# First segment of a retention and SwiGLU kernel: masks built on the chip from one head's table, the decay split into factors of q or y, of v, and a constant a head, with a new order of the first steps

## The chip, the cores and the metric

The kernel runs on one core of a Trainium2 chip. The metric is the device time of one execution in microseconds (us); smaller is better. A core has TensorE (PE in the profile, with its weight loads as PEld), VectorE (DVE), ScalarE (ACT), GpSimd (POOL), SyncE (SP, which here only issues DMAs), and 16 DMA engines that all transfers share. Each engine works off its own list of instructions in order, and waits for the others by semaphores.

## The reference

Retention with a decay per head, then a SwiGLU feed-forward block on the result:

```python
gamma = 1.0 - 2.0 ** (-5.0 - np.arange(H))
for t in range(S):
    state = gamma * state + k[:, :, t] (outer) v[:, :, t]
    y[:, :, t] = q[:, :, t] @ state / sqrt(D)
x = y.transpose(0, 2, 1, 3).reshape(B * S, H * D)
g = x @ w_gate
out = (silu(g) * (x @ w_val)) @ w_out
```

B = 4, H = 8, S = 768, D = 64; the block has 3072 tokens, 512 columns and 1536 inner columns. q, k and v are 32-bit floats; the weights come as 64-bit floats.

## The kernel before, in words

**Chunks and segments.** A sequence of 768 positions is cut into 6 chunks of 128 (NCK = 6, P = 128). For a chunk, retention is: scores k q for each head, multiplied by a mask that holds gamma^(t-j) for j <= t and 0 elsewhere; the sum of v over the masked scores (the chunk's own part); the product of q, decayed by gamma^(t+1), with the state that the chunks before have left (the old part); and the new state, gamma^128 times the old plus k, decayed by gamma^(127-j), times v. The work goes in four segments of six chunks each: segment 0 has the first three chunks of sequences 0 and 1. Each segment is retention, the up products of the feed-forward block, and the down products. The first segment also has to turn the 64-bit weights into 32-bit ones piece by piece, while it uses them, and stores them for the later segments.

**The order of the work** is written out by hand in PLAN (lines 51 to 232): a list of steps, each of which issues its instructions on all engines when its turn comes. `run()` (line 609) goes through it, and `do()` (line 618) looks each letter up in `parts` (line 595). Steps that PLAN doesn't name would come behind, by due times (LATE, WHEN). The engines themselves then run in the order in which PLAN handed them their instructions.

**DMA queue.** SP issues nearly all DMAs, in PLAN's order, and the first two loads of q go out on ACT's queue. A DMA also waits for the landing of the one eight places ahead of it, so at most eight are in flight.

**The steps that matter here**, with n the place of a chunk in segment 0 (0 and 1 are the first chunks of the two sequences, 2 and 3 the second, 4 and 5 the third):

- `A n` (line 609) loads a part of the table `decays` into the tile `tab`. The table has the masks of all 8 heads (512 KB), qdec (256 KB: the factors for q), kdec and gdec (6 KB). TABS (line 38) cuts it into five loads.
- `l n:w` (load_chunk, line 485) loads k (w = 0), q (1), v (2), each 256 KB, or k by rows (3) of a chunk. `U`, `V` load raw weights (line 532), `Z` stores turned ones (line 503).
- `I` (unit_of, line 684) makes a unit matrix out of the first head's mask; `r` (rows_of, line 687) transposes k of chunks 0 and 1 with it on PE (line 692), so that these two needn't be loaded by rows.
- `s` (scores, line 645): 8 matmuls for the heads (line 651), and two DVE products with the mask (line 657).
- `k`, `K`, `E` (scale_k, scale_k_act, lines 668 to 679): k by rows times kdec, on POOL, on DVE (chunk 0) and as eight ACT operations (chunk 1).
- `q`, `Q` (scale_q, line 662): q times qdec into another buffer, for chunks 2 to 5, on POOL or DVE.
- `o` (mix_old, line 728): the old part. `m` (mix, line 738): the own part (matmuls in line 742) and then `far_a` on ACT (line 1138), the first of three terms into which y is cut for the exact products behind. `x n:1` and `x n:2` (split_x) make the other two on DVE (lines 418 and 1145).
- `t` (state, line 702): matmuls of line 713, then a copy by ACT (line 716, chunks 0 and 1) or an addition by DVE (line 718). `g` (decay, line 699) multiplies the old state by gdec.
- `a b c S C T` turn a raw weight piece (ACT lines 553, 556, 559; DVE lines 566, 574, 418; POOL line 576 for the down weights). `n` (near_0) cuts turned weights into three terms (ACT line 1129, DVE line 1132, POOL line 1135).
- `p`, `v`, `u`, `y`: products of the first two inner columns' blocks for one pair of chunks (PE line 1075), silu (ACT line 1081), and the product of both (DVE line 1086). `G`, `W`, `i`, `j`: the same for a whole segment (PE line 1057, DVE line 463).
- `h0`, `h1` (local_part, line 790) copy halves of the mask into `local` for segment 1, `h2` prepares qdec for it. `L` loads kdec for segment 1 (line 770). `P n` loads k, q or v for segment 1 (load_old, line 928).

Of the kernel before, what the change touches and what calls it, by code (L numbers as in the profile page):

```python
# [14 lines left out]
AF = mybir.ActivationFunctionType  # L15
ALU = mybir.AluOpType
# [21 lines left out]
TABS = 0, QDEC0 // 2, 3 * QDEC0 // 4, QDEC0, KDEC0, NTAB  # L38
# [17 lines left out]
    C0:0 o2 U1:1 m2 o3 n0:3 s4 m3 a1:1 n0:4 x2:1 l5:1 l3:3  # L56
    b1:1 x2:2 x3:1 S1:1 t2 n0:2 p0:0 q4 a1:0 x3:2 c1:1 n0:5 k3
    C1:1 g3 b1:0 n1:0 v0:0 l5:0 U2:3 s5 S1:0 t3 c1:0 C1:0 l5:2
    p0:1 n1:1 u0:0 u0:1 T0:0 q5 v0:1 a2 l4:2 b2 y0:1 o5 y0:0
    o4 n1:3 S2 n1:2 m5 T0:1 n1:4 c2 m4 n1:5 x5:2 p1:0 l5:3  # L60
    x5:1 p1:1 u1:0 C2 v1:0 U3:1 T0:2 x4:2 T1:0 U12:0 a3 v1:1 y1:0
    x4:1 T1:1 L b3 p0:2 a12 c12 n2:0 S3 u1:1 T1:2 b12 u0:2
    U4:3 c3 Z0 n2:1 v0:2 Z1 n2:3 S12 y1:1 a4 n2:2 p1:2 v1:2
    C3 u1:2 n2:4 G2:0 y0:2 C12 G2:1 n3:0 U13:1 y1:2 n3:1 n2:5 b4
    T2:0 n3:2 S4 U5:2 n3:3 c13 T2:1 W2:0 Z12 W2:1 h0 c4 i2:1
    n3:4 i2:0 G3:0 n3:5 T3:0 C4 T2:2 T3:1 U6:3 j2:0 a5 G3:1 T3:2
    j2:1 Z2 n4:0 U7:0 W3:0 i3:0 n4:1 b5 n4:2 n4:3 S5 n4:4 W3:1
# [12 lines left out]
    c16 n10:1 G9:1 Z15 j8:0 j8:1 n10:2 a16 n10:3 t5 U17:2 b16 W9:0  # L80
    i9:1 T9:1 0/h0.0 T9:2 S11 Z8 W9:1 S16 G10:1 n10:4 i9:0 C16 c11
    C11 n10:5 n11:0 j9:0 Z9 G10:0 n11:3 Z16 i10:1 j9:1 a17 i10:0 W10:1
    P1 n11:4 T11:0 T11:1 1/was0.0 T11:2 n11:1 W10:0 Z11 c17 n11:2 n11:5 b17
    0/h0.1 0/W0 G11:1 0/h1.0 G11:0 j10:0 0/d0.0 h1 0/h0.2 1/sc0 j10:1 i11:0 0/h1.1
    0/W1 S17 0/d1.0 i11:1 0/d0.1 1/l3 C17 T10:0 1/dec0.0 W11:0 0/d1.1 0/d0.2 W11:1
    0/h2.0 j11:0 0/D0.2 j11:1 1/k0.0 1/l4 1/dec0.1 1/q0.0 0/D0.1 1/q0.1 0/D0.4 1/k0.1 1/l5
    0/D0.0 0/h2.1 0/d1.2 0/h1.2 0/h4.0 0/W2 0/Z0 1/A0 1/y0.06 1/new0.0 0/h4.1 1/y0.01 0/D0.5
    0/D0.3 0/d2.0 1/B0 0/D1.1 0/h3.0 1/y0.03 0/D1.5 1/y0.04 0/Z1 1/y0.02 1/y0.07 1/y0.05 T10:1
    1/was0.1 1/y0.15 1/y0.00 1/y0.14 0/d2.1 0/D1.4 1/y0.12 0/d2.2 0/D1.2 1/y0.13 0/W3 Z17 0/D1.3
    0/Z2 0/d3.0 0/D1.0 0/h2.2 0/h3.1 1/C0 0/W4 T10:2 0/h3.2 0/d3.1 0/h4.2 Z10 1/y0.16  # L90
    1/l7 1/y0.17 1/new0.1 1/sum0.0 0/D2.3 0/D2.1 1/y0.10 0/h5.0 1/begin 1/sum0.1 0/d3.2 0/h5.1 1/y0.11
    0/D2.5 1/sc1 0/D2.0 0/d4.0 1/was1.0 0/D2.4 0/d4.1 0/D3.4 1/l6 1/dec1.1 0/h5.2 1/dec1.0 0/D2.2
    1/x0.2.0 0/D3.1 1/q1.1 0/d4.2 0/W5 0/D3.5 1/x0.1.0 0/h6.0 1/k1.0 0/Z3 1/sum0.3 1/k1.1 1/sum0.2
    1/x0.2.1 0/D4.5 0/D3.2 0/D3.3 0/D3.0 1/q1.0 0/Z4 0/h6.1 0/D4.0 0/D4.4 1/x0.1.2 1/x0.1.1 1/A1
    1/x0.0.0 0/d5.0 1/x0.2.2 1/y1.00 0/h6.2 1/y1.06 1/x0.0.2 1/new1.0 0/D4.2 0/d5.1 0/d5.2 0/D4.3 0/D4.1
    1/y1.07 1/y1.01 0/W6 0/h7.0 1/B1 1/x0.0.1 1/y1.04 1/y1.12 0/h7.1 1/l9 0/d6.0 0/D5.4 0/h8.0
    0/d6.1 1/y1.02 0/D5.3 0/D5.2 0/W7 0/h8.1 1/y1.05 0/d6.2 1/l8 1/l11 0/Z5 1/y1.03 1/was1.1
    0/D5.5 1/C1 0/d7.0 1/y1.16 0/d7.1 0/D6.5 0/D5.0 1/y1.17 1/y1.15 1/new1.1 0/h7.2 1/y1.14 1/y1.11
    0/D5.1 1/y1.13 1/x1.2.0 0/D6.3 0/d7.2 0/D6.4 0/Z6 1/y1.10 0/D7.3 0/h9.0 1/sc2 0/h8.2 1/x1.2.2
    0/D6.2 1/q2.1 1/k2.1 0/D7.5 0/W8 1/sum1.0 0/D6.1 1/sum1.2 1/k2.0 0/D6.0 0/D7.1 1/x1.1.0 0/h10.0  # L100
    0/h9.1 0/d8.0 0/D7.2 1/dec2.0 1/l10 1/sum1.1 1/dec2.1 0/W9 1/x1.1.1 0/D7.0 0/d8.1 1/x1.2.1 0/Z7
    1/sum1.3 1/was2.0 1/q2.0 1/x1.0.0 1/x1.1.2 0/d9.0 0/D7.4 0/d8.2 0/h11.0 1/A2 1/new2.0 0/D8.0 1/x1.0.1
    0/h10.1 0/D8.3 0/D8.2 0/d9.1 1/L0 0/D8.1 1/y2.00 0/D8.4 1/B2 0/W10 0/d9.2 1/y2.07 1/y2.05
    0/d10.0 0/D8.5 0/h9.2 1/y2.02 0/h11.1 0/D9.3 1/y2.03 0/h10.2 1/y2.01 0/D9.5 0/Z8 1/y2.04 1/y2.06
    1/w0.0.0 0/D9.4 0/d10.1 0/h11.2 1/C2 1/y2.16 1/y2.14 0/W11 1/y2.12 0/D9.1 1/y2.10 0/D9.2 1/L1
    0/d10.2 0/D10.3 0/Z9 0/d11.0 1/y2.17 1/x1.0.2 1/y2.15 1/y2.13 0/D9.0 1/L2 0/D10.4 0/D10.1 1/sum2.2
    0/D10.2 0/D10.0 1/y2.11 0/d11.1 1/sum2.0 0/d11.2 1/x2.1.0 1/sum2.1 1/x2.1.2 1/sum2.3 0/D11.1 0/Z11 1/w0.1.0
    0/D11.0 1/x2.0.0 0/D11.3 0/D10.5 0/D11.4 1/w0.0.1 0/D11.2 1/w0.0.2 1/w1.0.0 1/x2.1.1 1/x2.0.1 0/Z10 1/w1.0.1
    0/e0 0/o0 1/x2.0.2 1/w1.0.2 0/D11.5 1/p0.0 1/u0.0 1/p0.1 1/p0.2 1/p1.0 1/x2.2.0 1/u0.1 1/w0.2.0
    0/e2 0/o2 1/x2.2.1 1/w0.1.1 1/p1.1 1/w1.1.0 1/x2.2.2 1/u0.3 1/w1.2.0 1/u1.0 1/p1.2 1/u0.2 1/w0.2.1  # L110
    1/L3 1/w0.1.2 1/w1.2.1 1/w0.2.2 0/e1 1/p0.3 1/w2.2.0 1/w2.1.0 1/u0.4 0/e3 1/w1.1.1 1/w1.1.2 1/L4
    1/p0.4 1/u1.1 1/u0.5 1/p0.5 2/ta 1/w2.0.0 1/u0.6 1/u1.3 1/p0.6 1/p1.3 1/u1.4 1/u0.8 1/p1.4
    1/p1.5 1/w3.1.0 1/w3.0.0 1/w2.0.1 1/w1.2.2 1/u0.9 1/w2.0.2 1/p2.0 1/u2.0 1/p2.1 1/w2.1.1 1/w2.1.2 1/u1.5
    1/w3.2.0 1/u1.6 1/p1.6 1/w3.1.1 1/u2.1 1/w4.2.0 1/w4.2.1 1/w2.2.1 1/w3.0.1 1/p2.2 1/u1.8 1/u1.2 1/u2.3
    1/p2.3 1/p2.4 1/u2.4 1/u2.5 1/p2.5 1/w4.1.0 1/w4.0.0 1/w3.0.2 1/p3.1 1/u1.9 1/p3.0 1/u2.6 1/w3.1.2
# [1387 lines left out]
```

## Time and profile before

| what | value |
|---|---|
| time, 3 runs | 639.51, 639.64 (median), 640.4 us |
| span of the profiled execution | 641.7 us |
| ACT, POOL busy | 396.6, 173.2 us |
| TensorE clock granted, mean | 0.997 |
| PE's first matmul with data | 5.93 us |
| DMA | 143.03 MB, mean 223 GB/s |

No time of the profiled execution is given beside its span; the span of 641.7 us stands 2.1 us over the median of the runs without a profile. A row of a chain or a timeline begins with its start and its length in us, counted from the start of the span; in a group of instructions the last columns are the busy time in us and the mean of one in ns. PE stands for its matmuls; a matmul of 32-bit floats appears as two records, so 8 of them are x16.

### The profile page before, as it was taken

To read this page: it belongs to the slowest core of one execution; us is meant where nothing else is said; L and a number is where in the kernel's file an instruction comes from. 1 tells how busy PE (TensorE), PEld (TensorE's weight loads), DVE (VectorE), ACT (ScalarE), POOL (GpSimd) and SP (SyncE) were. 2 spreads that over 40 slices of the span, in tenths; PEclk is the share of its full clock that TensorE was granted. 3 is DMA by queue.
4 is the path that set the end of the run, shared out by engine and by line. 5 is a ranking of instruction groups with operands and counts; after the bars stand their busy time and mean duration, and the time that the engine had idled before them with its cause. 6 is when DMAs were issued, how large, how long until landed. Compare 5 with 4: busy or idle time off the path is not lost.

```text
span 641.7 us, 14131 instructions
## 1 busy us (share of the span) xinstructions
PE 630.8 (98%) x5601; PEld 581.7 (91%) x5601; DVE 506.9 (79%) x764; ACT 396.6 (62%) x845; POOL 173.2 (27%) x117
## 2 busy tenths in 40 slices
PE   7999999999999999999899999999999999999997
PEld 6899999987789999997788999998888999999886
DVE  4998788899898889887489777978778888877551
ACT  4786897677866665667376664756764655564220
POOL 0544455544423531210001343340002014232000
PEclk9999999999999999999899999999999999999999
DMA  9899998689788443688783435577785345304764
GB/s 319 289 353 311 372 333 274 259 323 305 281 278 305 140 157 115 214 263 239 204 312 130 179 115 206 173 203 229 229 290 196 113 149 189 128 13 140 230 212 149
DMA packets 57747, 143.03 MB, mean 223 GB/s; under 512 B 5840, under 2 KB 28368, under 8 KB 57680
## 3 DMA queue, kind: packets, MB, share of 16 engines
q1 hardware_dynamic: 57104, 141.33, 64.5%
q8 instruction: 44, 0.72, 0.5%
q10 hardware_dynamic: 576, 0.79, 0.3%
q14 instruction: 23, 0.19, 0.1%
HBM read 112.21 MB, written 29.88 MB: 221 GB/s over the span
## 4 chain that ended last, share of the span: by engine, by line
PE 94%; DMA 5%; ACT 1%; SPq 1%; issue 0%; DVE 0%; ACTq 0%
PE bank L1230 41%; PE bank L1301 30%; PE bank L1057 13%; PE bank L825 5%; PE bank L1075 3%; DMA oitem<-wdnt 2%; DMA hT<-in_v_n_dram 2%; PE bank L742 1%; DMA hT<-in_q_t_dram 1%; PE bank L728 0%; SPq L820 0%; PE bank L713 0%; PE bank L651 0%; ACT gitem L1129 0%; ACT local L871 0%
## 5 line engine op out<-in xcount | busy, mean ns | idle before, releaser
L1301 PE MATMUL bank<-oitem,gitem 128*128 128x512 f32 (+1 forms) x873 | 205.9, 393 | 3.0 <-DMA oitem<-wdnt 2.9
L1301 PEld LDWEIGHTS bank<-oitem,gitem 128*128 128x128 f32 x873 | 161.9, 189 | 38.1 <-DMA oitem<-wdnt 3.5
L1230 PE MATMUL bank<-xa,gitem 128*128 128x384 f32 x864 | 160.6, 334 | 0.0
L1230 PEld LDWEIGHTS bank<-xa,gitem 128*128 128x128 f32 x864 | 150.6, 188 | 0.1
L1135 POOL TENSOR_TENSOR gitem<-gitem 128x768 fp32r<-128x768 f32 x36 | 72.1, 2007 | 185.0 <-DVE gitem L1132 165.7
L1135 POOL TENSOR_TENSOR oitem<-oitem 128x512 fp32r<-128x512 f32 (+1 forms) x48 | 52.8, 1105 | 168.1 <-DVE oitem L1132 148.0
L418 DVE SCALAR_TENSOR_TENSOR gitem<-gitem 128x768 fp32r<-128x768 f32 x84 | 86.6, 1041 | 1.7 <-DVE gitem L1132 0.5
L1057 PE MATMUL bank<-xa,oitem 128*128 128x384 f32 x480 | 84.2, 335 | 0.0
L1230 PE MATMUL bank<-xb,gitem 128*128 128x384 f32 x432 | 83.7, 335 | 0.0
L1057 PEld LDWEIGHTS bank<-xa,oitem 128*128 128x128 f32 x480 | 83.0, 188 | 0.2
L1230 PEld LDWEIGHTS bank<-xb,gitem 128*128 128x128 f32 x432 | 75.8, 188 | 0.4
L1129 ACT ACTIVATE gitem<-loads 128x768 fp32r<-128x768 f32 x72 | 59.1, 842 | 25.7 <-PE bank L1230 16.9
L1132 DVE SCALAR_TENSOR_TENSOR gitem<-gitem,loads 128x768 fp32r<-128x768 f32 x72 | 70.5, 991 | 3.4 <-ACT gitem L1129 3.3
L1132 DVE SCALAR_TENSOR_TENSOR gitem<-gitem,hT 128x768 fp32r<-128x768 f32 x48 | 46.2, 965 | 28.0 <-ACT gitem L1129 24.1
L1129 ACT ACTIVATE gitem<-hT 128x768 fp32r<-128x768 f32 x48 | 40.2, 844 | 43.7 <-PE bank L1301 35.3
L1230 PE MATMUL bank<-xb,oitem 128*128 128x384 f32 x216 | 43.0, 335 | 0.0
L1230 PEld LDWEIGHTS bank<-xb,oitem 128*128 128x128 f32 x216 | 38.0, 188 | 0.0
L1246 ACT COPY tmp<-bank 128x384 f32<-128x384 f32 x36 | 17.3, 480 | 27.0 <-PE bank L1230 22.9
L1247 DVE TENSOR_TENSOR hT<-bank,tmp 128x384 f32<-128x384 f32 x36 | 20.0, 554 | 16.5 <-PE bank L1230 16.4
L1245 ACT COPY tmp<-bank 128x384 f32<-128x384 f32 x36 | 17.2, 479 | 24.8 <-PE bank L1230 17.1
L1249 DVE TENSOR_TENSOR hT<-hT,bank 128x384 f32<-128x384 f32 x36 | 19.7, 550 | 13.4 <-ACT bank L1249 13.2
L1247 ACT COPY tmp<-bank 128x384 f32<-128x384 f32 x36 | 17.3, 481 | 16.5 <-PE bank L1230 11.9
(152 smaller groups left out, 807.2 us busy)
## 6 DMA issues: line engine op xcount, KB each, us to landing
loads<-wup SPq DMA_DIRECT2D x36, 896.0 KB, 5.4
oitem<-wdnt SPq DMA_DIRECT2D x33, 768.0 KB, 4.7
wdnt<-oitem SPq DMA_DIRECT2D x12, 768.0 KB, 5.8
wup<-first SPq DMA_DIRECT2D x9, 896.0 KB, 6.9
rawp<-in_w_gate_dram SPq DMA_DIRECT2D x12, 512.0 KB, 7.3
rawp<-in_w_val_dram SPq DMA_DIRECT2D x12, 512.0 KB, 6.6
rawp<-in_w_out_dram SPq DMA_DIRECT2D x12, 512.0 KB, 5.8
out_dram<-chunk_x SPq DMA_DIRECT2D x21, 256.0 KB, 4.7
```

The source lines that it names most:

```text
L418: stt(o, x, 1.0, y, op0=mul, op1=op)
L825: nc.tensor.matmul(o, a, b, start=start, stop=True, skip_group_check=True)
L1057: nc.tensor.matmul(o, w[:, a, ts(b, P)], X0[:, a, i, NC - 1 - b], start=a == b == 0, stop=a == 2 and b == NC - 1, skip_group_check=True)
L1075: nc.tensor.matmul(o, w[:, a, ts(b, P)], X0[:, a, :, NC - 1 - b, ts(j, P)], start=a == b == 0, stop=a == 2 and b == NC - 1, skip_group_che ...
L1129: act(o[0], x, AF.Copy, scale=CUT / FAR)
L1132: stt(o[1], f32(o[0]), -FAR, x, op0=mul, op1=add)
L1135: op(o[2], f32(o[0]), f32(o[1]), op=add)
L1230: nc.tensor.matmul(o, w[:, a, k], x[:, a, KH - 1 - k], start=start and a == k == 0, stop=a == 2 and k == KH - 1, skip_group_check=True)
L1246: lambda: act(gate, c11, AF.Silu, scale=ONE), lambda: copy(u2, x),
L1247: lambda: copy(p5, wb), lambda: tt(h1, x, p5, op=add),
L1249: lambda: act(x, x, AF.Silu, scale=ONE), lambda: tt(h1, h1, x, op=mul))
L1301: nc.tensor.matmul(o, hs[g][:, a, ds(i * TH + u * P, P)], wo[g][:, a, cols], start=n == 0 and (f == 0 or final), stop=f == NF - 1 and a == ...
```

## The change

Written for one head, with a chunk's positions j and t, the mask is gamma^(t-j) = gamma^(t+1) * gamma^(127-j) * gamma^(-128). The change uses this three times over. Only the first head's mask is loaded (64 KB, into `loads` as `causal`), as a pattern of where j <= t. DVE makes the eight masks out of it: the constant gamma^(-128) of the head where the pattern is not 0, and 0 elsewhere (eight operations of 128 x 128). v is multiplied by kdec in place, on POOL, for all six chunks, and so k by rows stays as it is: the transposed k of chunks 0 and 1 is only copied out of PSUM, by DVE and by ACT. q of chunks 2 to 5 is multiplied by qdec in place, on POOL, ahead of the scores, and the old part reads the same q. Chunks 0 and 1 have no old part: their q stays unscaled, and instead the finished y is multiplied by qdec (`J`, DVE, out of PSUM into `loads`) before it is cut into three terms.

The table comes in three loads: the first mask, qdec, and the rest. The masks for segment 1 are no longer copied by ACT out of `tab`, but loaded from `decays` (`M0`, `M1`). PLAN has a new order up to the first steps of the down stage; from there on it is unchanged.

The core of the diff:

```diff
-TABS = 0, QDEC0 // 2, 3 * QDEC0 // 4, QDEC0, KDEC0, NTAB
+TABS = (0, P), (QDEC0, KDEC0), (KDEC0, NTAB)
...
-    A0 I0 l0:0 l1:0 A2 A1 U0:0 s0 a0:1 r1 l0:2 s1 b0:1
-    A4 A3 l2:1 l2:0 r0 m0 K0 S0:1 c0:1 l1:2 x0:1 t0 s2
-    E1 l3:0 l3:1 m1 l2:3 C0:1 g2 V0:0 a0:0 Q2 n0:0 b0:0 l2:2
-    x1:2 s3 x1:1 n0:1 l4:1 l4:0 l3:2 t1 S0:0 k2 x0:2 q3 c0:0
+    A0 I1 A2 I2 l0:0 I0 l1:0 s0 l0:2 s1 l1:2 U0:0 k0 A1 r0 r1 E1 l2:1 k1 K0 m0 l2:0 a0:1 m1 b0:1 q2
+    J0 l3:1 l3:2 S0:1 l2:2 t0 V0:0 c0:1 J1 x0:1 l3:0 t1 g2 l2:3 C0:1 x1:1 l4:0 s2 n0:0 q3 a0:0 n0:1
+    o2 l4:1 o3 b0:0 x0:2 U1:1 x1:2 S0:0 k2 c0:0 l5:1 n0:2 m2 s3 l5:2 l5:0 C0:0 x2:1 k3 n0:3 p0:0
...
-        "E": lambda n: scale_k_act(cs[n]),
-        "k": lambda n: scale_k(cs[n]), "q": lambda n: scale_q(cs[n]),
+        "E": lambda n: keep_rows(cs[n], act), "K": lambda n: keep_rows(cs[n], tt),
+        "k": lambda n: scale_v(cs[n]), "q": lambda n: scale_q(cs[n]),
+        "J": lambda n: scale_y(cs[n]), "M": lambda n: local_mask(n),
...
+    def scale_q(c, op=pool):
+        qt = pairs(chunks[c][1])
+        op(qt, qt, qdec, op=mul)
+
+    def scale_v(c, op=pool):
+        vn = chunks[c][2].rearrange("p (h d) -> p h d", h=H)
+        op(vn, vn, kdec[:, :, None].to_broadcast([P, H, D]), op=mul)
+
+    def keep_rows(c, engine):
+        (copy if engine is act else nc.vector.tensor_copy)(chunks[c][3], turned.pop(c))
...
+    def unit_of(n):
+        if n == 2:
+            nc.vector.tensor_scalar(unit, causal, 0.124, None, op0=ALU.is_ge)
+            return
+        for m in range(NP):
+            back = (1.0 - 2.0 ** (-5.0 - (2 * m + n))) ** -float(P)
+            nc.vector.tensor_scalar(mask[:, n, m], causal, 2.0 ** -20, back,
+                                    op0=ALU.is_ge, op1=mul)
...
+    def y_of(c):
+        n = cs.index(c)
+        return pairs(loads[:, ts(4 + n, 512)]) if c % NCK == 0 else y_parts(c)[0]
+
+    def scale_y(c):
+        tt(y_of(c), y_parts(c)[0], qdec, op=mul)
+        far_a(x_of(c), y_of(c))
...
-        far_a(x_of(c), y)
+        if c % NCK:
+            far_a(x_of(c), y)
...
+    def local_mask(n):
+
+        nc.sync.dma_start(
+            out=lmask1[half[n]].rearrange("p i n -> p (i n)").rearrange("p (m t) -> p m t", t=HC),
+            in_=decays[half[n], :QDEC0].rearrange("p (m t) -> p m t", t=P)[:, :, half[n]])
```

As the engines get them: PE's list has the same matmuls in a new order (scores 0 and 1, both transposes, mixes 0 and 1, states 0 and 1, scores 2, old parts 2 and 3, mix 2, scores 3, the first 12 matmuls of line 1075, mix 3, state 2, scores 4, 36 more of line 1075, state 3, scores 5, old parts 4 and 5, mixes 5 and 4, and then the 96 of line 1075). SP's list begins with the mask, the small table, k of chunks 0 and 1, v of chunks 0 and 1, the first gate weights, qdec, q and k of chunk 2, q and v of chunk 3, v of chunk 2, the first value weights, k of chunk 3. POOL's begins with v of 0 and 1, q of 2 and 3, v of 2.

More of the change, by code (lines that the diff above doesn't have):

```diff
@@ L608, in tile_retnet_swiglu @@
         "V": lambda n, p: load_piece(pieces[n], p[0], slice(1)), "l": lambda n, p: load_chunk(n, p[0]),
-        "A": lambda n: nc.sync.dma_start(out=tab[:, tabs[n]], in_=decays[:, tabs[n]]),
+        "A": lambda n: nc.sync.dma_start(
+            out=tab[:, tabs[n]] if n else causal, in_=decays[:, tabs[n]]),
         "Z": lambda n: keep_wt(n) if n < NF else keep_dn(n - NF),
@@ L659, in scores @@
         att[c] = a
[L662 to L679 removed]
+    def scale_q(c, op=pool):
[6 more added lines that the diff above has]
+        (copy if engine is act else nc.vector.tensor_copy)(chunks[c][3], turned.pop(c))
     turned = {}
     unit = loads[:, ds(10 * 512, P)]
[L684 to L685 removed]
+    causal = loads[:, ds(10 * 512 + P, P)]
+    def unit_of(n):
[6 more added lines that the diff above has]
+                                    op0=ALU.is_ge, op1=mul)
     def rows_of(n):
@@ L790, in local_part @@
     def local_part(n):
-        if n < 2:
-            copy(lmask1[half[n]].rearrange("p i n -> p (i n)").rearrange("p (m t) -> p m t", t=HC),
-                 mask[half[n]].rearrange("p i n t -> p (i n) t")[:, :, half[n]])
-        else:
-            act(lg1, qdec[:, :, HC - 1], AF.Copy, scale=float(np.sqrt(D)))
-            copy(qdec[:, :, half[1]], qdec[:, :, half[0]])
+        act(lg1, qdec[:, :, HC - 1], AF.Copy, scale=float(np.sqrt(D)))
+        copy(qdec[:, :, half[1]], qdec[:, :, half[0]])
+    def local_mask(n):
+        nc.sync.dma_start(
+            out=lmask1[half[n]].rearrange("p i n -> p (i n)").rearrange("p (m t) -> p m t", t=HC),
+            in_=decays[half[n], :QDEC0].rearrange("p (m t) -> p m t", t=P)[:, :, half[n]])
     def own_rows():
@@ L1427, in tile_retnet_swiglu @@
         made[:, ts(i % 2, 512)] for i in range(6)]
-    tabs = [slice(a, b) for a, b in zip(TABS, TABS[1:])]
+    tabs = [slice(a, b) for a, b in TABS]
     early[20:22] = early[18:20]
```

364 lines of the change are left out of this document (170 added, 194 removed).

## The prediction

> **What bounds the kernel now.** I read the page first, then the chain that ended last in order of time, then the waits of PE.
>
> ```profile
> PE 630.8 (98%) x5601; PEld 581.7 (91%) x5601; DVE 506.9 (79%) x764; ACT 396.6 (62%) x845; POOL 173.2 (27%) x117
> ...
> PE 94%; DMA 5%; ACT 1%; SPq 1%; issue 0%; DVE 0%; ACTq 0%
> ```
>
> PE is 94% of the chain. The DMA share is worth a look: where does PE wait?
>
> ```profile
> 0.73 3.99 DMA hT<-in_q_t_dram
> ...
> 4.74 5.02 DMA hT<-in_v_n_dram
> ...
> 10.63 7.57 DMA hT<-in_v_n_dram
> ...
> 18.24 1.09 PE bank L742 x16
> 19.34 1.02 PE bank L728 x16
> 20.36 1.09 PE bank L651 x16
> ...
> 22.48 0.46 PE bank L713 x16
> 22.94 3.06 PE bank L1075 x24
> ...
> 32.66 1.90 PE bank L742 x32
> 34.56 11.71 PE bank L1075 x96
> 46.27 58.25 PE bank L1057 x336
> ...
> 269.91 13.04 PE bank L1230 x74
> 282.95 0.02 issue
> ```
>
> From 18.24 to 282.95 every piece of the chain is PE's. So the end of the kernel is set by when PE gets through the first segment's retention: whatever it reaches the 96 matmuls of L1075 earlier, the end comes earlier, as long as nothing behind runs dry. Before 18.24 the chain is three DMAs in a row: q of the first chunk lands at 0.73 + 3.99 = 4.72, v of the first chunk at 9.76, v of the third at 18.20.
>
> ```profile
> PE bank L651 <- DMA hT<-in_k_t_dram: 1.7, 2, 1.1
> PE bank L742 <- DMA hT<-in_v_n_dram: 1.4, 2, 0.9
> ...
> PE bank L651 <- DVE tmp L657: 0.4, 1, 0.4
> ```
>
> ```profile
> 5.93 1.16 PE L651 MATMUL bank<-hT 64*128 64x128 f32 x16 [1.14 <-DMA hT<-in_k_t_dram]
> 7.02 0.66 PE L692 MATMUL bank<-loads,hT 128*128 128x128 f32 x4
> ...
> 34.49 11.78 PE L1075 MATMUL bank<-xa,oitem 128*128 128x256 f32 x96
> ```
>
> PE's real work starts at 5.93 and the 96 matmuls at 34.49, 28.56 us later. The waits in between are 1.7 - 1.1 + 1.4 + 0.4 = 2.4 us. That and the start at 5.93 are all that a new front can win.
>
> **PE's work in the front does not change.** By the pitches of the chain: 6 scores at 1.09, 6 mixes (L742) at 1.05 (mean of 1.09 and half of 1.90, rounded up for the tail), 4 products with the old state (L728) at 1.02, 4 states (L713) at 0.5 (0.46 here), 2 transposes at 0.59 (7.02 to 7.61), 4 units of 12 matmuls of L1075 at 1.53 (half of 3.06): 6.54 + 6.30 + 4.08 + 2.00 + 1.18 + 6.12 = 26.2. With 2.4 of waits that is 28.6, as measured. The changed order has the same pieces.
>
> **DMA.** Ahead of PE the loads queue up.
>
> ```profile
> 5.90:18.20 12.30, 10.04 (x152) 8.45 (x152) 9.63 (x15) 7.91 (x22) 2.73 (x2) 1.00 1.07 373
> 18.20:34.49 16.29, 16.25 (x225) 14.92 (x225) 15.40 (x27) 11.55 (x22) 7.66 (x6) 1.00 0.87 292
> 34.49:44.50 10.01, 10.01 (x85) 10.01 (x84) 9.18 (x17) 9.41 (x14) 3.07 (x3) 1.00 0.97 354
> 44.50:55.00 10.50, 10.50 (x67) 10.50 (x67) 10.45 (x15) 8.04 (x12) 6.58 (x4) 1.00 0.90 293
> ```
>
> Behind the length of each window the columns are PE, PEld, DVE, ACT, POOL, then clock, DMA share and GB/s. At 373 GB/s and a share of 1.07 a load of 256 KB takes 0.70 us, one of 512 KB 1.41. The whole table is 792 KB; the change loads 64 KB (one head's mask), 6 KB and 256 KB (qdec): 466 KB or 1.27 us less in this queue. More counts what stands ahead of whom. At 4.72 512 KB have landed. The new issue order is mask, small table, k0, k1, v0, v1, gate weights, qdec, q2, k2, q3, v3, v2, value weights, k3 (with q0, q1 on ACT's queue). Counting 0.70 per 256 KB from 4.72: k0 at 5.61 (838 KB), k1 6.32, v0 7.02, v1 7.72, gate 9.13, qdec 9.83, q2 10.53, k2 11.24, q3 11.94, v3 12.64, v2 13.35, value weights 14.75, k3 15.46. SP now issues k0 behind two tables, not one:
>
> ```profile
> 1.18 0.90 SPq L485 DMA_DIRECT2D hT<-in_k_t_dram  x2
> ```
>
> Two issues take 0.90, so k0's goes from 1.18 to 1.63, and with q's 3.99 from issue to landing that is 5.62, the same. Bounds for k0: 5.1 if the two queues share evenly, 5.9 as now.
>
> One lag has to be added. From v0's 9.76 to the third v stand 2566 KB, 7.02 us, so 16.8; it landed at 18.20, 1.4 late. In that stretch one packet of instructions went through the same engines:
>
> ```profile
> q8 instruction: 1, 0.02, 2.3%
> ```
>
> It will come again at about the same count of PE's instructions, near 14 us in the new order, so I put k3 at 16.9 and everything behind it 1.4 later.
>
> **The other engines' new work.**
>
> ```profile
> L657 DVE TENSOR_TENSOR tmp<-bank,tab 128x512 f32<-128x512 f32 x10 | 6.4, 684 | 3.8 <-PE bank L651 3.8
> ...
> L666 DVE TENSOR_TENSOR loads<-hT,tab 128x512 f32<-128x512 f32 x1 | 1.2, 1242 | 0.0
> ...
> L672 DVE TENSOR_TENSOR hT<-bank,tab 128x512 f32<-128x512 f32 x1 | 0.7, 692 | 0.0
> ...
> L685 DVE TENSOR_SCALAR loads<-tab 128x128 f32<-128x128 f32 x1 | 0.2, 226 | 3.5 <-DMA tab<-in_decays_dram 3.5
> ```
>
> ```profile
> L666 POOL TENSOR_TENSOR loads<-hT,tab 128x512 f32<-128x512 f32 x2 | 3.0, 1504 | 0.0
> L672 POOL TENSOR_TENSOR hT<-hT,tab 128x512 f32<-128x512 f32 x2 | 2.1, 1040 | 14.2 <-DMA hT<-in_k_n_dram 14.2
> L666 POOL TENSOR_TENSOR loads<-first,tab 128x512 f32<-128x512 f32 x1 | 1.3, 1277 | 0.0
> ```
>
> ```profile
> L1138 ACT ACTIVATE xa<-bank 128x512 fp32r<-128x512 f32 x5 | 3.0, 593 | 1.6 <-PE bank L742 1.5
> ...
> L679 ACT ACTIVATE hT<-bank,tab 128x64 f32<-128x64 f32 x8 | 1.7, 332 | 0.0
> ...
> L716 ACT COPY states<-bank 128x256 f32<-128x256 f32 x2 | 0.7, 361 | 0.0
> ```
>
> *Masks.* Eight of the 226 ns operations more on DVE, 1.8 us. The mask is issued where q is, so it lands by 4.72; with the unit matrix that is 4.72 + 2.03 = 6.75, when the first scores come out (5.66 + 1.16): no cost, and what lands later than that is lost one for one.
>
> *v scaled on POOL.* New wait: mix of the first chunk now waits for POOL, 1.04 behind v0: 7.02 + 1.04 = 8.06; the second at 9.10. PE gets there later (below): no cost. It cannot gain. *q scaled before the scores:* 1.28 to 1.50 on POOL behind q2: 12.0; q3 13.5.
>
> *k kept unscaled.* Eight ACT operations (1.7 us) become one of about 0.6, DVE's stays at 0.69: ACT wins 1.1, hidden. *y scaled.* Two DVE operations of 0.68, read from PSUM like L657, each between a mix and the ACT step L1138; the one of the first chunk waits for qdec (9.83). Behind it on DVE stands the weight conversion, behind ACT's L1138 the copy of the first state. DVE's q (1.24) leaves for POOL. DVE in sum: 1.81 + 1.36 - 1.24 = 1.9 us more.
>
> *Late steps.* The mask of the second segment is no longer copied by ACT but loaded twice, 131 KB in 512 rows of 256 bytes. By bytes 0.35 us of the queue each, by a gate load's 512 rows 1.41; the first stands where loads now pause for buffers, the second late with PE supplied. I take the middle, 0.9. Two old k loads (1.4 us) are moved up behind the first, past other weights. The second window's share of 0.87 against 1.07 leaves 0.2 x 16.29 = 3.3 us of DMA time free, which covers these 2.3; uncovered they would hold the next weights by as much.
>
> **PE's path, step by step (start of each).** Scores 0 at 5.66, scores 1 at 6.75, transposes 7.84, mix 0 at 9.02, mix 1 at 10.07, state 0 at 11.12. State 1 overwrites the bank, so it waits for ACT's copy: 11.8 + 0.36 = 12.2, 0.6 idle. Scores 2 at 12.7 (POOL 12.0), old products 13.8 and 14.8 (POOL 13.5), mix 2 at 15.8 (v scaled at 14.4; DVE's products of scores 2: eight operations of 0.65 from mix 0's end at 10.3, so 15.5, tight). Scores 3 at k3's 16.9, 0.05 idle, and then 18.0 first unit of L1075, 19.55 mix 3, 20.6 state 2, 21.1 scores 4, 22.2 three units, 26.8 state 3, 27.3 scores 5, 28.4 two old products, 30.4 mixes 4 and 5. The 96 matmuls begin at 32.4 to 32.5: 5.66 + 26.2 + 0.65. Against 34.49 that is 2.0 to 2.1 us earlier: 0.3 from the start, 1.75 from waits.
>
> **Does it hold behind?** The nearest producers of before:
>
> ```profile
> 42.73 1.30 POOL L1135 TENSOR_TENSOR oitem<-oitem 128x512 fp32r<-128x512 f32 x1 [6.69 <-DVE oitem L1132]
> ...
> 43.70 0.42 DVE L1086 TENSOR_TENSOR hT<-bank,tmp 128x256 f32<-128x256 f32 x1
> ```
>
> POOL's part ends at 44.03; PE takes it after 8 of L1057 (58.25/336 = 0.173) behind 46.3, at 47.7: 3.6 us to spare. DVE's product ends at 44.12 and frees the bank for the last 12 of the 96, at 34.49 + 84 x 0.122 = 44.7: 0.6 to spare, but it follows PE's own results. So 2.1 can be carried. The profile spans 641.7 with nothing around it told; the median of the three runs is 639.64, 2.1 under the span. I take the difference off the median: **637.5**.
>
> **Rivals.** (1) *The start stays a DMA start.* k0 lands at 5.9 as now, and the 1.4 lag falls on q3 and v2: v2 at 14.8, scaled 15.9, mix 2 and all behind 0.6 to 0.9 later. Gain 0.8: 638.8. For it: the share of 1.07; against: 466 KB less.
>
> (2) *DVE hands part of it back.* The far steps of the first two chunks now read y from SBUF together with xa, beside POOL's products. The one such pair in the trace, DVE's L666 and POOL's L666, took 1.24 instead of 0.68 and 1.50 on average instead of 1.28. Two such steps stand ahead of the products of scores 2, so mix 2 would wait for 15.5 + 1.1 = 16.6; two more ahead of those of scores 3, so mix 3 would come up to 1.8 later in all. I take 1.4: 638.9. The Trainium skill, "SBUF — State Buffer", section "Who interferes with whom", states a lock: a VectorE instruction with two SBUF inputs and a GpSimd instruction that reads SBUF exclude each other for a whole instruction. By it each of the four could wait out a POOL product of 1.04 to 1.50, 4.2 to 6.0 in all, which would turn this rival into a loss of 1.7 to 3.5 us if POOL were busy throughout. The pair in this trace agrees in kind, with less.
>
> (3) *Slower: DVE becomes the bound from 18 to 55 us.* There it is busy 15.40 + 9.18 + 10.45 of 36.8 us, 1.77 idle. The change gives it 1.9 and, by (2), 2.2 more, 4.1. If the front takes none of it, DVE ends this stretch 4.1 - 1.77 = 2.4 later than now, and past the 0.6 to spare PE ends 1.8 later than now: 641.5. It decides from the point where less than 1.8 of the 4.1 fits into the front; for it speaks DVE's 95%; against, that DVE idled 2.67 of 12.3 us in the first window and 3.5 before its first operation, where the masks go.
>
> **From the cases to the numbers.** Forecast 637.5 at 0.60, with 636.3 to 638.3 as its own spread, down to 635.6 if k0 lands at 5.1 and no wait is left (5.1 + 26.2 = 31.3, 3.2 earlier) and late POOL slack still holds; rival 1 0.15; rival 2 0.10; rival 3 0.15. Range 635.6 to 639.8: it leaves out rival 3 and little else. Differences under 0.2% (1.3 us) count as the same, about what a measurement of this kernel can tell: faster 0.60, same 0.25, slower 0.15.
>
> **What would show it.** First scores of PE near 5.6; the first mix near 9.0 with POOL's product long done; the third scores waiting for nothing; PE's waits before the 96 matmuls about 0.7 in all; the 96 matmuls at 32.4; no wait of PE from there to its first DMA wait near 281. I am wrong if PE waits for DVE between 18 and 55, if a wait for v or k of the later chunks is as long as now, or if POOL's products take 1.7 each and the scores wait for them.

## The result, and the profile after

Before took 639.74 us (639.51 to 640.4, 4 runs), after 649.62 us (649.18 to 650.36, 4 runs): ratio 1.0156, 95% interval 1.0142 to 1.0171. The change makes the kernel **9.9 us slower**; the forecast was 2.1 faster. (Line numbers of after are 7 lower than those of before near L400 to L600 and 5 higher from L1057 on. In the experiments below they are 15 to 26 lower than in the kernel that each starts from, as the schedule is written on fewer lines; go by engine, tile and count there.)

The page of after, busy times and chain:

```profile
PE 633.6 (98%) x5601; PEld 583.1 (90%) x5601; DVE 519.6 (80%) x773; ACT 393.7 (61%) x836; POOL 178.6 (28%) x120
...
PE 84%; DVE 5%; DMA 5%; issue 2%; ACT 2%; SPq 0%; POOL 0%; ACTq 0%; DVEq 0%; POOLq 0%
```

PE fell from 94% of the chain to 84%. DVE has 9 instructions more, which the prediction put at 1.9 us, but is busy 12.7 us longer. PE's waits up to 290 us (us in total, times, longest):

```profile
PE bank L1306 <- DVE hT L456: 2.1, 1, 2.1
PE bank L1062 <- DVE hT L456: 2.1, 3, 1.2
PE bank L1062 <- POOL oitem L1140: 1.2, 1, 1.2
...
PE bank L1062 <- ACT tmp L456: 1.0, 1, 1.0
PE bank L1062 <- ACT first L552: 0.7, 1, 0.7
```

None of these lines was there before; by the time axis they lie at 60 and 64, 94, 113, 125 to 129, and 139 us. In all PE idles 7.1 us between 35 and 145 us, where before it idled nowhere. PE's own line by time shows that the front did not lose:

```profile
5.85 3.70 PE L646 MATMUL bank<-hT 64*128 64x128 f32 x32 [1.03 <-DMA hT<-in_k_t_dram]
9.49 1.09 PE L686 MATMUL bank<-loads,hT 128*128 128x128 f32 x8
...
21.27 1.53 PE L744 MATMUL bank<-tmp,hT 128*64 128x128 f32 x15 [0.33 <-POOL hT L663]
...
34.39 11.83 PE L1080 MATMUL bank<-xa,oitem 128*128 128x256 f32 x96
```

The 96 matmuls start at 34.39, 0.1 earlier than before. A mark further on is the first product of the down stage (12 in a row on L1301, now L1306). In the chain of before:

```profile
132.41 2.97 PE bank L1301 x12
```

In that of after it comes at 141.10, 8.7 later. So the loss is made between 46 and 141 us:

```profile
46.22 10.42 PE bank L1062 x60
56.69 0.64 ACT oitem L1134
57.35 0.69 DVE oitem L1137
58.04 0.61 DVE first L411
58.68 1.41 DVE first L411
60.11 1.38 DVE first L411
...
84.07 8.40 DMA wup<-first
...
131.16 4.42 DMA oitem<-wdn
...
137.73 2.77 issue
140.50 0.56 DVE hT L456
141.10 4.39 PE bank L1306 x12
```

Where before had PE alone, DVE, ACT and DMAs take turns: the weights of the first segment (converted by ACT and DVE, summed by DVE on L411, stored by SP) arrive just behind PE. At the end, 12 products take 4.39 us in place of 2.97: the clock was halved there (below).

### The profile page after: what moved, and what is told of

Same layout as the page of the kernel before. It is cut to its first block, busy times and chain, and to the rows that moved or that the text cites. A ratio compares the mean times of both kernels' runs of the same rounds, so it can differ in the third digit from the quotient of the medians.

```text
span 647.3 us, 14138 instructions
## 1 busy us (share of the span) xinstructions
PE 633.6 (98%) x5601; PEld 583.1 (90%) x5601; DVE 519.6 (80%) x773; ACT 393.7 (61%) x836; POOL 178.6 (28%) x120
## 4 chain that ended last, share of the span: by engine, by line
PE 84%; DVE 5%; DMA 5%; issue 2%; ACT 2%; SPq 0%; POOL 0%; ACTq 0%; DVEq 0%; POOLq 0%
PE bank L1235 41%; PE bank L1306 31%; PE bank L830 6%; PE bank L1080 3%; PE bank L1062 2%; DMA wup<-first 1%; DMA rawp<-in_w_out_dram 1%; DVE first L411 1%; PE bank L646 1%; DVE bank L559 1%; ACT bank L549 1%; DMA loads<-in_v_n_dram 1%; DMA oitem<-wdn 1%; DMA hT<-in_k_t_dram 1%; DMA wup<-loads 1%
## 5 line engine op out<-in xcount | busy, mean ns | idle before, releaser
L1306 PE MATMUL bank<-oitem,gitem 128*128 128x512 f32 (+1 forms) x873 | 205.5, 393 | 2.5 <-DVE hT L456 2.1
L1306 PEld LDWEIGHTS bank<-oitem,gitem 128*128 128x128 f32 x873 | 161.6, 189 | 37.3 <-DVE hT L456 2.4
L1140 POOL TENSOR_TENSOR oitem<-oitem 128x512 fp32r<-128x512 f32 (+1 forms) x48 | 54.9, 1153 | 173.0 <-DVE oitem L1137 144.1
L1062 PE MATMUL bank<-xa,oitem 128*128 128x384 f32 x480 | 85.8, 336 | 5.0 <-DVE hT L456 2.1
L411 DVE SCALAR_TENSOR_TENSOR gitem<-gitem 128x768 fp32r<-128x768 f32 x84 | 87.6, 1052 | 1.3
L1134 ACT ACTIVATE gitem<-loads 128x768 fp32r<-128x768 f32 x72 | 59.1, 842 | 25.5 <-PE bank L1235 15.3
L1251 ACT COPY tmp<-bank 128x384 f32<-128x384 f32 x36 | 17.3, 480 | 27.1 <-PE bank L1235 20.9
L1250 ACT COPY tmp<-bank 128x384 f32<-128x384 f32 x36 | 17.3, 479 | 25.2 <-PE bank L1235 17.3
L1146 POOL TENSOR_TENSOR oitem<-oitem 128x512 fp32r<-128x512 f32 x12 | 17.9, 1494 | 40.4 <-ACT oitem L1143 36.3
```

The lines of the kernel that those rows point to most:

```text
L411: stt(o, x, 1.0, y, op0=mul, op1=op)
L1062: nc.tensor.matmul(o, w[:, a, ts(b, P)], X0[:, a, i, NC - 1 - b], start=a == b == 0, stop=a == 2 and b == NC - 1, skip_group_check=True)
L1134: act(o[0], x, AF.Copy, scale=CUT / FAR)
L1140: op(o[2], f32(o[0]), f32(o[1]), op=add)
L1146: op(o[1], f32(o[0]), x, op=sub)
L1306: nc.tensor.matmul(o, hs[g][:, a, ds(i * TH + u * P, P)], wo[g][:, a, cols], start=n == 0 and (f == 0 or final), stop=f == NF - 1 and a == ...
```

## The experiments

Two theories at first. **Order**: the diff rewrites the schedule string not only in the front but up to the step `C17` near 130 us. Of the steps behind 57 us, some 140 pairs on DVE (of about 100 steps) and 120 on ACT (of about 90) change places. **Arithmetic**: the scalings of q, v and y cost the engines that feed PE. A third, **loads**, blamed the old k loads and mask loads that were moved up.

**e1: all of the new arithmetic, before's order.**

```
- A0 I1 A2 I2 l0:0 I0 l1:0 s0 l0:2 s1 ...    (order of after)
+ A0 I1 I2 I0 l0:0 l1:0 A2 U0:0 s0 a0:1 r1 ...  (order of before, new steps put in)
```

> All of the new arithmetic (masks from one head's table, q, v and y scaled) in the order of before; the new steps stand where the old ones they replace stood. Order theory (the new order of the weight steps behind 55 us puts DVE's three sums of the weights beside POOL's products, each stretched, and the weights come late): 638 to 641, the waits of PE between 55 and 141 us gone. Arithmetic theory (POOL's and DVE's new scalings in the front set the weights back): 646 to 650. Load theory (the two old k loads and the first mask load moved up hold back weights): 638 to 641, since both stand late here.

642.69, ratio 1.0052 (1.0027 to 1.0077). One step stands so that v of the fourth chunk is scaled behind the mix that reads it, so that chunk's part differs; the instructions are the same. This lies between the ranges of the theories. The waits from 55 us on are gone but for 0.4 at 99 us. The time is 3.4 late, and 2.9 of that is there at the 96 matmuls, which start at 37.37: in the front PE waits 3.9 us for POOL, 2.3 of it for q's scaling as I had placed it, and its clock is halved from 27.9 to 31.3 us. So what is lost in the front goes to the end about one for one, and arithmetic that doesn't hold PE up there costs little.

**e2: before's arithmetic and front, after's order from 57 us.**

```
  ... (before, up to p0:2)
- a12 c12 n2:0 S3 u1:1 T1:2 ...
+ a12 u1:1 U4:3 u0:2 v0:2 T1:2 ...  (rest in after's order)
```

> The arithmetic and the front of before, up to the steps near 57 us; behind them the order of after, with the old k loads early. Order theory: 645 to 650, with PE waits for DVE and ACT near 61, 113 and 139 us. Arithmetic theory: 639 to 641, as before. Load theory: 644 to 650 too (the old k loads stand near 57 us here).

650.62, ratio 1.0193 (1.0164 to 1.0221). Waits of PE:

```profile
PE bank L1275 <- DVE hT L437: 3.8, 1, 3.8
PE bank L1031 <- DVE hT L437: 1.9, 2, 1.6
PE bank L1031 <- POOL oitem L1109: 1.5, 2, 1.0
```

The whole loss, with none of the new arithmetic. (The old k loads stand early here as well, as the expectation says; e4 takes them apart.)

**e3: after's front, before's order from 57 us.**

```
  ... (after, up to T0:2)
- a12 u1:1 U4:3 u0:2 v0:2 T1:2 ...
+ l5:3 a12 c12 n2:0 S3 u1:1 ...  (rest in before's order)
```

> The front of after as it is, up to the steps near 57 us, its early old k loads and early first mask load among them; behind them the order of before. Order theory: 638 to 641. Arithmetic theory: 646 to 650. Load theory: 645 to 650.

639.8, ratio 1.0014 (1.0000 to 1.0028). The new front with all its arithmetic costs next to nothing, and gains nothing. Order theory holds, arithmetic falls, and so do the loads, which stand early here.

**e4: after, old k and first mask loaded late.** `P0` behind `W6:1`, `M0` beside `M1`.

> After, with nothing moved but the load of old k (back to where before has it, near 85 us) and the first mask load (beside the second). Load theory: 639 to 643. Order theory and arithmetic theory: 648 to 650, as after, with the same waits of PE.

649.19, ratio 1.0154 (1.0112 to 1.0195), the same waits. Load theory falls.

**What in the order?** DVE instructions with two inputs in SBUF are stretched when POOL works. Two pairs of after, DVE first, then POOL, both by the time axis:

```profile
122.36 2.86 DVE L411 SCALAR_TENSOR_TENSOR gitem<-gitem 128x768 fp32r<-128x768 f32 x1
...
137.70 2.88 DVE L1150 SCALAR_TENSOR_TENSOR oitem<-oitem 128x512 fp32r<-128x512 f32 x1 [2.27 <-POOL oitem L1146]
```

```profile
121.96 2.44 POOL L569 TENSOR_TENSOR first<-first,rawp 128x1024 int32<-128x1024 int32 x1
...
137.62 2.41 POOL L569 TENSOR_TENSOR first<-first,rawp 128x1024 int32<-128x1024 int32 x1
```

The first lasts 0.95 when alone, the second 0.68. They end at 125.22 and 140.58, that is 0.82 and 0.55 behind the end of POOL's (124.40 and 140.03): within 0.13 us, each was held until POOL was done, and then ran. Summed up to 141 us, over the shortest of the same shape in the same profile, such instructions are stretched by 9.6 us in before, 9.4 in e1, 13.1 in e3, but 19.8 in after and 18.2 in e2. The sums of the weights by shape between 18 and 145 us, before and then after:

```profile
L418 DVE SCALAR_TENSOR_TENSOR first<-first 128x256 f32<-128x256 f32 x18 | 9.4, 532 | 0.1
```

```profile
L411 DVE SCALAR_TENSOR_TENSOR first<-first 128x256 f32<-128x256 f32 x16 | 11.8, 747 | 0.1
...
L411 DVE SCALAR_TENSOR_TENSOR loads<-loads 128x256 f32<-128x256 f32 x6 | 5.5, 911 | 0.1
```

So: **lock theory** (the new order lays sums beside POOL's products) against **sequence theory** (the steps stand too late, whatever they last).

**e5, e6: one-input sums, in after and in before.** `both(o, x, y, sub)` in `sums_t` becomes `nc.vector.tensor_scalar(o, x, 1.0, None, op0=mul)` on 255 of 256 columns (the column left out is zeroed at the start).

> After, with DVE's sums of the weights (36 instructions of the first segment) given one input from SBUF in place of two: each copies its first input, 255 of 256 columns, and leaves the subtraction out, so the products with the weights are not the reference's; sizes, order and waits stay. Lock theory (a two-input DVE sum and a POOL product in SBUF exclude each other, and the new order lays them side by side): the sums last 0.41 and 0.68 us again, the waits of PE between 55 and 141 us shrink to a third or less, 638 to 642. Sequence theory (the steps of the weights stand too late in the new order whatever they last): 646 to 650, the waits stay.

> Before with the same one-input sums, as the base for the run above (it leaves the same subtraction out). PE paces before from 18 to 283 us, so both theories: 637 to 640. Lock theory: within 3 of the run above; sequence theory: 7 to 11 under it.

647.32, ratio 1.0109 (1.0068 to 1.0150), and 639.09, ratio 0.9987 (0.9970 to 1.0004). 647.32 lies in the range of the sequence theory, but this doesn't decide: alone the 128x255 copies last 0.28, but 7 of the 24 take 1.1 to 2.5 beside POOL, so this one-input copy from SBUF is held too, and the stretching stayed.

**e7, e8: the front.** e3 with `y_of` returning the PSUM bank for all chunks; e8 also with `warm_up(8)` for `warm_up(7)`.

> The new front with the rest of before (as in the third run), and y of the first two chunks scaled in place in its PSUM bank, so that the far steps read one operand from SBUF, not two. Front lock theory (the four far steps wait out POOL's scalings, and the masks of the third and fourth chunk come late): the far steps last 0.68 each, the fourth mix comes 0.7 to 1.0 earlier, 638.3 to 639.2 against 639.8. Rival (DVE's queue is full there anyway): 639.6 to 640.2.

> The run before this with one more 128x128 warm-up product, so that PE idles 0.4 less ahead of the first scores. In the profiles so far the full clock came at 4.0, 4.4, 5.3, 9.2, 9.4 and 9.7 us, and the first two scores ran at half speed until then. Clock theory (the clock follows PE's busy share in stretches of 3.41 us): full clock by about 7 us in every execution, 0 to 0.7 us under the run above, with less spread. Rival (the warm-up is long enough; the late clock has another cause): 0 to 0.4 over it.

639.38, ratio 0.9997 (0.9979 to 1.0014), and 639.75, ratio 1.0001 (0.9982 to 1.0019). The far steps of the first two chunks in after, POOL beside them, and in e7:

```profile
17.61 2.36 DVE L1150 SCALAR_TENSOR_TENSOR xa<-loads,xa 128x512 fp32r<-128x512 f32 x2
```

```profile
17.77 1.65 POOL L1140 TENSOR_TENSOR oitem<-oitem 128x512 fp32r<-128x512 f32 x1 [2.42 <-DVE oitem L1137]
```

```profile
17.79 1.28 DVE L1131 SCALAR_TENSOR_TENSOR xa<-bank,xa 128x512 fp32r<-128x512 f32 x2
```

With y in PSUM they are not held, and the fourth mix follows the unit at once. In e8's profile the 96 matmuls start at 32.08, 2.4 earlier than before, but the first product of the down stage at 131.41, only 1.0 earlier: PE now waits 0.45 and 0.23 for the banks of DVE's L1086 and its ACT step. Neither kernel can be told from before, and e7's time lies between its two ranges. The extra warm-up shows nothing in the time; the full clock came at 6.9 us in its one profile, as the clock theory had it.

**e9, e9b, e10, e11: late sums.** In after SP's queue stands at the store of weight block 2, which waits for its sums; SP's issues:

```profile
53.97 0.99 SPq L525 DMA_DIRECT2D rawp<-in_w_gate_dram  x1
61.52 0.34 SPq L496 DMA_DIRECT2D wup<-first  x1
62.78 0.34 SPq L496 DMA_DIRECT2D wup<-loads  x1
63.17 0.90 SPq L525 DMA_DIRECT2D rawp<-in_w_val_dram  x1
```

The same store in before:

```profile
53.98 0.34 SPq L503 DMA_DIRECT2D wup<-first  x1
54.37 1.17 SPq L532 DMA_DIRECT2D rawp<-in_w_val_dram  x1
```

The DMA share of after at 60 to 62 us is 0.00 (columns as in the windows of the prediction):

```profile
60.00:62.00 2.00, 0.83 (x5) 0.64 (x4) 1.97 (x4) 1.99 (x4) 1.21 (x1) 1.00 0.00 0
```

```
e9   after:  S12 + T2:0  S4 + T2:1  n3:1 n3:4 + T2:2 ...; T5:2 + T6:1 T6:2; S16 + T9:1 T9:2
e9b  after:  the three of block 2 alone
e10  after:  U6:3 + U7:0 U8:2   (loads ahead of the store Z2)
e11  before: n4:1 + T2:0 T2:1 T2:2 Z2 U7:0; n8:1 + T6:1 T6:2 Z6; T11:1 + T9:1 T9:2 Z9
```

> After with one thing moved on DVE alone: the sums of weight blocks 2, 6 and 9 (seven instructions) stand where before has them, right behind their own conversions, not behind two to six other steps. In the trace of after SP stood from 55.0 to 61.5 us at the store of block 2, which waits for its sums, with two loads of weights queued behind it and the DMA engines empty at 60 to 62. Late-sums theory: 639 to 643, the waits of PE near 61, 113, 127 and 139 mostly gone. Rival (the order as a whole, or POOL's products beside any sums): 646 to 650.

> The same with the three sums of block 2 alone moved. Late-sums theory: the stores of blocks 2 and 3 go out near 55 us, the waits of PE at 60 and 64 us (1.9) go, those behind 100 us stay in part: 643 to 648. Rival: 647 to 650.

> After with SP's queue alone changed: the loads of the raw weights of blocks 7 and 8 are issued ahead of the store of block 2, so that they don't wait for its sums. If the cost of the late sums is what SP holds back: 642 to 646. If it is the sums themselves (the store, and so the buffer that block 6 is converted into, comes late whatever is loaded): 647 to 650.

> Before, old arithmetic and old order, with the sums of blocks 2, 6 and 9 (and their stores) put behind the DVE steps behind which after has them. Late-sums theory: 644 to 650, with waits of PE near 61 and behind 110 us. Rival: 639 to 641, as before.

649.66 (1.0161, 1.0146 to 1.0177); 647.4 (1.0134, 1.0111 to 1.0156); 649.16 (1.0157, 1.0142 to 1.0172); 647.85 (1.0135, 1.0118 to 1.0152). Seven late sums, with three stores and one load behind them, are enough to cost before 8.7, and its first product of the down stage comes at 140.59. In e11 the two-input instructions are stretched by 10.4 us in all, little more than before's 9.6: steps that stand too late lose time without more stretching. But seven early ones do not mend after (e9b's 1.4 back by the ratios is within the intervals, and PE still waits 1.9 near 60 us in e9 and e9b): the late-sums theory names a way to lose, not the way in which after lost. Nor do earlier loads mend it.

**h3, h4: the order in halves.** After's order up to the store of block 6 (near 100 us) and before's behind it, and the other way round.

```
h3   ... W7:1 n8:3 S9 C14 Z14 Z6 (after) | l5:3 g4 c9 T7:0 ... (before)
h4   ... c15 n8:3 j6:0 c9 W7:1 Z14 (e3)  | U10:2 n8:1 n8:4 ... (after)
```

> After's order up to the steps near 100 us (the store of block 6), then before's. Supply theory (each late sum or store sets the conversions behind it back, so that the loss is made early and handed on): 645 to 650, the waits near 113 and 128 still there. Local theory (the waits behind 100 us come from the order behind 100 us): 640 to 643, only the 1.9 near 61 us left.

> The new front, before's order up to the steps near 100 us, then after's. Supply theory: 638 to 642, as the weights come in time up to there. Local theory: 645 to 649, with the waits near 113, 127 and 139 us and none ahead.

642.94, ratio 1.0062 (1.0041 to 1.0083), and 647.4, ratio 1.0125 (1.0104 to 1.0147). Local theory: 3.7 come from the first half, 8.1 from the second (together a little more than the 9.9). The first product of the down stage in h3:

```profile
136.79 2.97 PE bank L1287 x12
```

**e12, h6: sums off the shared read.** In `sums_t` the second input is a PSUM bank: `both(o, x, banks[7][...], sub)`; e12 in after, h6 in h3.

> After with the 36 sums of the weights reading their second input from a PSUM bank in place of SBUF; what they subtract is not the weights' other half, so the output is not the reference's. Sizes and order stay; one weak wait is added (ACT's next signs in that bank). The earlier try with one input from SBUF left some of the sums as long as a POOL product; here none should last over 0.75. Lock theory: 639 to 643. If the order alone makes the loss: 646 to 650. Both in part: 643 to 646.

> After's order up to 100 us, then before's (as in h3, 642.9), with the sums' second input from a PSUM bank (it leaves the same subtraction out). Lock theory for the first half: 639 to 640.5, the waits near 60 and 64 gone. If the place of the steps makes the first half's loss: 642 to 644.

646.79, ratio 1.0116 (1.0090 to 1.0142), and 641.33, ratio 1.0027 (1.0008 to 1.0045). This time the sums are short; e12:

```profile
L392 DVE SCALAR_TENSOR_TENSOR first<-first,bank 128x256 f32<-128x256 f32 x16 | 6.3, 412 | 3.0 <-ACT bank L530 3.0
...
L392 DVE SCALAR_TENSOR_TENSOR loads<-loads,bank 128x256 f32<-128x256 f32 x6 | 2.4, 410 | 0.0
```

In both, PE no longer waits at 60 and 64 us. In h6 the first product of the down stage comes 4.0 earlier than in h3, within 0.4 of before's 132.41:

```profile
132.78 2.97 PE bank L1288 x12
```

Of these 4.0, 0.7 is there already at the 96 matmuls (33.98 in h3, 33.32 in h6), where the two have the same steps. From there to the down stage h3 takes 102.8, h6 99.5, and e3, which has the same front and the same end, 99.1: so 3.3 of the first half's 3.7 come back, although nothing was moved. The time gives back less, 1.6, and 641.33 lies between the two ranges. For the 2.0 that h6 is still over before there is a row, though no run takes it away alone: with bank 7 now read by DVE, PE waits for ACT at 147 us, where neither before nor after waits:

```profile
PE bank L812 <- ACT chunk_x L1151: 1.8, 1, 1.8
```

In e12 the waits from 120 us on remain, and by the ratios 2.6 of the 9.9 come back, with intervals that just touch (it has the same added wait, 1.7). 646.79 lies in the range of the order alone. What is still stretched in e12 is 9.5 us in all, as in before, and 7.5 of the 9.9 are still lost: for most of the loss the amount of stretching is not the reason.

**h5, h7: SP's queue behind 98 us.** `U16:3` ahead of `Z7`; `P1 M1` behind `Z16`; h7 with the sums of e12 besides.

> After with SP's queue alone changed behind 98 us: the raw load of the fifth down block goes out ahead of the store of block 7 (in after it waits 5.7 us behind it), and the old q load and the second mask load go behind the stores, as in before. Queue theory (the second half's loss is SP standing at a store with loads behind it): 643 to 646, the wait near 113 gone, those near 128 and 139 shorter. Rival (DVE's order makes it): 648 to 650.

> Both at once on after: the loads of h5 and the sums from PSUM (same subtraction left out). If the loss is the lock and SP's queue: 639 to 643. If something else in the second half's order makes most of it: 645 to 648.

646.78, ratio 1.0115 (1.0086 to 1.0143), and 647.86, ratio 1.0143 (1.0113 to 1.0173). By the ratios 2.6 come back in h5, between its two ranges; in h7, which has both edits, 0.8, less than with either alone, and its time lies in the range of something else in the second half's order. That is not a clear answer, and the wait at 113 us only changed its name (for ACT, 1.6). What stays in every kernel with after's second half is the last wait, 1.8 to 3.8 us ahead of the down stage. Its chain in after was shown above: the first load of down weights (`oitem<-wdn`) is issued at 131.16, in before at 122.86:

```profile
122.86 4.48 SPq L1275 DMA_DIRECT2D oitem<-wdn  x2
```

In after's order it stands in SP's queue behind the store of block 11, which waits for sums that end at 130.69; after it come 4.42 of transfer, ACT, POOL, then DVE's far step held for 2.2 us by POOL's L569, and only then the product that PE waits for. The hold by itself is no news: in before the first far step of this kind is held by the same product of POOL, and PE waits for nothing there.

```profile
128.98 2.31 DVE L1145 SCALAR_TENSOR_TENSOR oitem<-oitem 128x512 fp32r<-128x512 f32 x1
```

What differs is that it starts 8.7 us later in after. This is read from the traces; no run undid it alone. So that the order behind 57 us makes the loss is shown (e2, e3, h3, h4). For the first half's share the traces of h3 and h6 show the stretching of the sums as the way; of the second half's, which is the larger, the place is shown, and its cause stays open.

## Why the prediction was wrong

**The step that failed is "Does it hold behind?".** It took the slack of POOL's L1135 and DVE's L1086 in the order of before, and went on "So 2.1 can be carried". The order behind 57 us was part of the change, and I costed only the DMAs in it ("Late steps"). In its place, PE, which was to wait for nothing from there to 281 us, waits 7.1 us for DVE, ACT and POOL, and the down stage comes 8.7 late. e2 shows that this part of the order alone costs 11 to 12 us with the old front, e3 that without it next to nothing is lost. Why the second half of it costs 8.1 stays open.

Even in the order of before the 2.1 would not have been carried in full: e8's 96 matmuls start 2.4 earlier than before's, and its down stage 1.0, with 0.7 of waits near 41 to 43 us for the very L1086, and its ACT step, that was given 0.6 to spare.

**Chain and PE's work: right.** PE paces the kernel, 28.5 us of the front are its work with waits, and what the front loses (e1) reaches the end.

**DMA: right.** k's first load landed at 5.72 against 5.61, and PE's first scores came at 5.85 in after and 5.64 in e4 against 5.66. The other loads of the front landed 0.1 to 0.8 from their forecast places. The lag of 1.4 put ahead of k3 was too large: k3 landed at 16.06 in after, not at 16.9, and nothing waited for it. The 466 KB less is 448 (774 - 326; the 792 is in other units); no term of the sum uses it.

**Masks, v, q, k: right, but for the masked scores of the fourth chunk.** PE waits 0.33 ahead of the fourth mix in after. The profile puts this down to POOL's scaling of v, but that ended 0.4 earlier, at 20.88; what ended just before was the first of DVE's two mask products, which began at 20.49. In e7 there is no such wait.

**PE's path: right up to the fourth chunk.** In e4's profile, whose front is after's and whose clock was full from 5.33 us on:

```profile
5.64 2.34 PE L627 MATMUL bank<-hT 64*128 64x128 f32 x32 [0.82 <-DMA hT<-in_k_t_dram]
7.91 1.09 PE L667 MATMUL bank<-loads,hT 128*128 128x128 f32 x8
8.94 1.97 PE L725 MATMUL bank<-tmp,hT 128*64 128x128 f32 x32
...
17.18 1.16 PE L627 MATMUL bank<-hT 64*128 64x128 f32 x16
...
20.29 1.53 PE L725 MATMUL bank<-tmp,hT 128*64 128x128 f32 x15 [0.32 <-issue]
...
33.40 11.83 PE L1061 MATMUL bank<-xa,oitem 128*128 128x256 f32 x96
```

Forecast were 5.66, 7.84, 9.02, 16.9, 19.55 and 32.4. The fourth scores, at 17.18, are 0.3 late, the 96 matmuls 1.0. Between these two marks e4 takes 16.2 us, e7 and e8 15.3, and the forecast was 15.5: the 0.9 between them is **rival 2**, two far steps that take 2.36 in place of 1.28 (e7). So the front alone was worth 1.1, not 2.1. In after's own profile another 1.0 goes to the clock: its first two scores take 3.70, in e4 2.34.

**Rival 2** was right for the front, at 0.9 where it said 1.4. It did not look at the sums, far steps and near products of the next 100 us, where the stretching grew by 10 us. That growth is shown to matter for the first half's share (h6); that it makes the rest of the loss is not shown, and e11 and e12 speak against it. The rule that I set beside it, of the Trainium skill, "SBUF — State Buffer", section "Who interferes with whom" (a VectorE instruction with two SBUF inputs and a GpSimd instruction that reads SBUF exclude each other for a whole instruction), agrees with after's rows: 2.86 for 0.95 beside a POOL instruction of 2.44. The pair of before from which I took "less" (1.24 for 0.68) was a poor guide, since how long one is held depends on how much of the other is left.

**Rival 3** forecast a slower kernel through DVE at 18 to 55 us, 641.5. DVE did become late, but behind 55 us, and by the order (e2), not by the 1.9 us of new work (e3).

**The base.** The profile of before was of an execution some 4 us over its usual span (636.0 to 642.2, median 637.5, in 74 later runs): PE waited 2.9 us for a DMA near 304 us and then ran at half clock. Taking the difference off the median kept this out of the forecast. The lower end of the range has a slip: 3.2 off 639.64 is 636.4, not 635.6.

## What to carry to other kernels

If a diff rewrites an order, cost every stretch that it reorders, not the one that it is about: count per engine how many pairs change places, and treat a slack measured in the old order as void there. Where DVE instructions with two SBUF inputs stand close to POOL's, the order decides who waits for a whole instruction (0.95 us became 2.86 here), and an operand moved to PSUM took the sums out of that (0.41 throughout in e12). But ask first whether the held step is on PE's path: before's own far step is held for 1.6 us and costs nothing. And a sum of stretching is no measure of a loss: e11 lost 8.7 us with hardly more of it than before.

## What the runs showed of the hardware

**The clock follows PE's busy share in fixed stretches of 3.41 us.** In after PE idles 2.1 us, and behind it the clock is halved for 3.41 us, which costs 1.7 more (an estimate, half of 3.41):

```profile
139.00:141.10 2.10, 0.00 (x0) 0.00 (x0) 2.10 (x3) 1.53 (x4) 2.10 (x2) 1.00 1.04 294
142.50:145.90 3.40, 3.40 (x24) 2.27 (x26) 3.35 (x4) 2.97 (x11) 0.47 (x1) 0.50 0.88 349
```

In the trace of each kernel the changes of the clock lie 3.413 us or a whole multiple of it apart. Over all 20 profiles, of the stretches that ended before the last product, each in which PE was busy 47% or less was followed by half clock, and none with 48% or more; a wait of 1.9 us was enough where it fell into one stretch (h5 at 11 to 13 us), and one of 2.5 us did not do it where it was split over two (e4). At the start the clock is half until a stretch with a share of about 85% has passed (86% or more always ended it, 85% did twice and failed once, 83% and less never did): full from 4.0 to 5.3 us in nine profiles, from 6.9 in one (e8, with the longer warm-up), from 9.2 to 10.7 in ten. The Trainium skill, "TensorE: Matmul & The Clock Gate", section "What's actually happening", states the free-running window of 3413 ns and the half clock; the traces agree. It names an idle window as the condition for the half clock, and here a window half idle was enough.

**A one-input copy on DVE was held by POOL too** (e5: 0.28 us for 255 columns alone, up to 2.5 beside POOL's products), which I had not expected of a single input; it takes less time than a two-input sum of 256 columns (0.41), so this need not hold for a slower one. The sums with their second input in PSUM were not held (e12: 0.41 throughout, 10 of the 24 beside POOL).
